# Thresholded attention and a mixer on one core: the queue of double score steps is run over the border between two couples of head pairs, with new ranks for the planner

## The chip, the cores and the metric

The kernel runs on one core of one Trainium2 chip. The metric is the device time of one execution in microseconds (us). A core has TensorE (PE in the profile, with its weight loads as PEld), VectorE (DVE), ScalarE (ACT), GpSimd (POOL) and SyncE (SP), each with its own instruction queue, worked off in order, and DMA queues. PSUM, where PE writes, has eight banks; the kernel names six of them as two "trios" and the last two bank 6 and bank 7.

## The reference, cut to what matters

```python
# q, k, v: (8 batches, 8 heads, 576 rows, 64)
scores = q @ k.T / 8
thresh = max(scores, axis=-1) - tau                       # tau = 0.02
attn = exp(where(scores >= thresh, scores, -1e9) - max(scores))
attn = attn / (sum(attn, axis=-1) + 1e-9)
x = (attn @ v), heads side by side                        # (8, 576, 512)
u = x + (x^T @ U @ V)^T                                   # U: 576 x 32, V: 32 x 576
out = u + relu(u @ w_ch1) @ w_ch2                         # 512 -> 2048 -> 512
```

## The kernel before

**How the work is tiled.** Two heads of one batch make a head pair p; there are 4 in a batch and 32 in all. A *step* is 128 rows of queries against all 576 keys, for both heads of a pair, so it makes two tiles of 128x576. A pair has 576 rows, which is four steps and a half; the two halves of neighbouring pairs p and p+1 (p even) share one step, i = 4. So a couple of pairs has nine steps, and there are 16 couples, 144 steps and 288 tiles.

**What a step does.** `scores` (L574, products at L587) multiplies q and k in fp32 with the array split into quadrants of 64x64, into the two trios. `weigh` (L615, L616, DVE) reads a tile from PSUM, scales it by -1/8, keeps the copy `s_sb` and the row minimum m. `threshold` (L632, ACT) makes the threshold of both tiles, `exponential` (L639, ACT) the exponentials, `select` (L644, L646, DVE) compares, multiplies and sums. The row is completed (`twin`, L664, POOL) and turned, by a DMA (`turn_w`, L670, from SP) or on PE for some early tiles (`turn_pe`, L677, copied out at L687). Then, per pair, `value_tasks` multiplies with v (`product`, L746, L750, L754), joins the parts (L787 ACT, L791 DVE), divides (L798, POOL; for the first four pairs L775 on DVE), goes through the low-rank pair U, V (L811, L826, L833, L874, L881) and turns the result for the mixer (by DMA at L854, by PE at L848 and L896 with copies at L864 and L901).

**Single and double steps.** `score_tasks(*steps)` takes one step or two. One step writes four of the six banks of the trios, two steps write all six (`KEPT`, L149). The `PIECES` (L410) give where the columns are cut, so the instructions of a step are 16 matmul passes in either case. Up to pair 1 all steps are single (`LONE = 2`); from the second couple on the first of nine steps is single and the other eight make four doubles. That is 9 + 15*5 = 84 groups.

**The mixer.** After every fourth pair `mixer_tasks(b)` adds the two layers of batch b: `up` (L930, 16 tasks of four 512-column products), `rest` (L946, for the 64 rows left over of two batches, 128 columns), the rectifier (`relu`, L920, ACT), and `down` (L963, 16 products for each 128 rows of output), then `finish` (L975, DVE) and the stores (L986 to L992, SP and ACT).

**What sets the order.** Nothing runs when it is written: every piece of work is a task with an engine, an estimated cost, dependences and a number of PSUM banks, and `Order.run` (L214 on) places all of them once, at build time, engine by engine. Among the tasks of an engine that could start within a short patience of the first, it takes the one of lowest rank. The rank of most tasks is the planned time at which they became ready plus `OFF[name][phase]`, where the phase is counted by `PHASES = (1, 2, 3, 4, 5, 6, 8, 28)` from the pair's number. Mixer products have a due number instead (`DUE[b]` and what L928 on adds to it): when so many score steps have been placed, they go ahead of all others; until then they are taken only where nothing else is ready. `HOLD` says how long banks are kept free for the next score group. Where PE would stand idle for over 0.45 us of the plan, filler products (L421) of no use to the result are placed, which keep PE's clock up; there are 84 of them.

The loop that lists the tasks stands at the end of the kernel (L1047 on): for every couple it prepares both pairs (loads and turns of q and k), adds the nine score steps, then the values of both, then a mixer where a batch is complete.

Of the kernel before, what the change touches and what calls it, by code (L numbers as in the profile page):

```python
# [81 lines left out]
NT = 5  # L82
# [5 lines left out]
LONE = 2  # L88
# [5 lines left out]
DUE = (461, 86.25, 1468.5, 516.25, 1049.25, 748, 134.75, 1357.5)  # L94
# [33 lines left out]
class Order:  # L128
# [19 lines left out]
    HOLD = (61.76, 61.61, 6.12, 44, 94.32, 94.08, 76.76, 0.01, 9.57)  # L148
# [4 lines left out]
        "copy_main": (25.53, 63.74, -194.99, 34.77, -69.14, 17.14, -324, 37.67, -35.45),  # L153
        "copy_rest": (6.5, -40.06, -14.53, 24.12, -4.13, -20.91, -46.23, 54.32, -95.65),
        "copy_tt": (-16.03, -64.1, 20.85, -110.66, 55.87, 62.18, -42.53, -53.37, -25.08),
        "copy_u": (89.47, -53.33, 162.09, -74.19, 7.13, 9.51, -102.11, -20.31, -73.82),
        "copy_u4": (-5.3, -56.82, -16.18, -6.54, 49.93, -37.52, 64.79, -22.2, -18.99),
        "copy_w": (75.7, -4.79, -22.58, 20.52, -4.75, 68.84, -1.46, 27.15, 10.06),
        "down": (52.39, 32.35, 33.69, 38.82, 7.25, -27.49, 1.69, 19.34, 131.97),
        "exponential": (61.02, 15.66, 97.71, -26.58, 23.56, 95.43, 116.8, 90.08, 11.21),  # L160
        "finish": (-53.17, -45.71, 51.42, 30.79, -14.22, -26.29, 28.78, 16.33, -75.01),
        "first": (-56.79, 75.89, 0.92, -55.7, 35.86, -3.48, 9.68, 53.63, 1.2),
        "high": (-129.72, -35.78, 31.87, -6.58, 48.08, -20.33, -28.95, -46.46, 84.01),
        "inverse": (46.71, -32.89, 54.08, 22.1, 122.91, 38.13, 143.23, 39.39, -23.27),
        "join": (2.19, 36.38, 69.81, -65.72, -28.72, -7.68, -26.75, 24.75, -3.5),
        "load": (14.89, -38.6, -1.87, -55.09, 439, 169.52, 202.43, 266.17, -64.61),
        "low": (23.82, 3.88, -45.02, 6.6, -28.12, -60.17, -87.19, -43.1, 26.46),
        "low4": (64.5, 130.96, 545.14, -26.82, 13.94, -59.21, 35.95, 265.72, -23.85),
        "low_part": (30.38, 13.98, -26.01, -41.71, 130.31, 109.34, -20.82, -133.07, -1.88),
        "low_rank": (-57.69, 16.1, -2.98, 31.4, -60.74, 41.37, 38.61, 8.08, -35.05),  # L170
        "make": (-18.31, -192.85, -81.78, -52.29, 6.69, -18.25, 12.16, -35.09, 27.21),
        "narrow": (5.95, 39.32, -9.64, -6.72, 1.46, 29.45, -10.31, 45.69, -47.12),
        "narrow_u": (-45.99, -94.08, -136.7, -16.38, -46.01, -113.33, 15.29, 42.82, -0.02),
        "narrow_u4": (2.02, -41.08, 15.16, 12.95, 69.79, 35.67, -44.1, -54.14, 56.42),
        "norm": (60.22, 26.73, 14.75, 16.35, 28.89, -20.28, -16.45, 55.02, 19.4),
        "product": (-38.14, -97.33, -17.17, 18.14, -78.98, 56.88, 40.12, 68.18, -110.66),
        "relu": (44.72, -2.34, -31.3, -83.46, 20.06, -116.77, 10.32, 4.5, -36.91),
        "rest": (64.49, 74.43, 34.29, 18.04, -20.78, -41.41, -55.22, -17.62, 44.45),
        "scores": (-2.16, -56.15, 42.01, -69.96, -15.23, -44.76, 4.79, -16.69, -3.93),
        "select": (-41.99, 29.22, -2.51, 135.03, 570.07, 400.28, 184.53, 231.57, 188.34),  # L180
        "send": (43.87, 17.75, 5.67, -19.7, -14.51, -9.84, 285.3, 70.92, -48.56),
        "send_u": (54.83, -57.33, -16.36, 177.37, 12.48, 121.89, 19.74, 60.45, 25.84),
        "spread": (-216.88, 63.66, -12.54, -9.53, -23.32, -1.29, -122.3, 43.34, 63.38),
        "spread4": (12.62, -19.59, -18, 54.22, -34.85, 61.33, -24.98, -50.63, -66.91),
        "spread_v": (-113.69, -64.83, 6.03, 44.27, 73.51, -47.79, -27.38, 65.24, 2.79),
        "sum_u": (-64.77, 3.32, 13.18, 117.53, -78.44, -9.21, 87.33, 127.21, -64.36),
        "sum_u4": (-96.51, 65.77, 2.32, 38.3, 44.64, 21.12, -125.78, 37.98, 23.47),
        "sums": (195.64, 23.57, 47.14, -31.56, 10.32, -16.1, 35.4, 4.49, -58.98),
        "threshold": (-37.94, -91.24, -43.1, -296.86, 94.89, 36.19, 66.3, 1.07, 12.5),
        "turn4": (-36.19, -43.45, 5.14, 7.01, 54.44, -61.28, 52.57, 29.57, -92.54),  # L190
        "turn_main": (0.34, 20.57, 26.79, -161.06, 126.25, -30.36, -38.23, -14.86, -5.97),
        "turn_pe": (-0.48, -21.65, -184.33, 36.36, -95.83, 51.55, 181.65, 20.16, -43.63),
        "turn_rest": (-5.99, -37.64, -0.75, 52.43, -6.2, -61.13, -8.69, -94.49, -32.06),
        "turn_u": (-85.8, -3, -69.47, -45.79, 74.76, -7.02, 3.37, 12.83, 72.77),
        "turn_w": (45.6, -1.19, -137.3, 47.86, -48.09, 10.25, -28.07, -30.73, 72.41),
        "twin": (32.78, -132.71, -13.72, -15.07, -38.22, -14.87, -64, 49.79, 55.76),
# [125 lines left out]
def kernel(  # L322
# [725 lines left out]
    for p in range(0, NP, 2):  # L1048
# [3 lines left out]
        n = 0  # L1052
        while n < 9:
            two = p >= LONE and n
# [44 lines left out]
```

## Time and profile before

| what | value |
|---|---|
| median of 5 runs | 603.32 us (602.52 to 606.07) |
| profiled execution, its own time | 603.32 us |
| its span in the profile | 601.5 us |
| PE, first start and last end in the span | 3.3 and 596.9 us |
| last store issued | 597.6 us |
| granted clock of PE | 0.998 |
| HBM read and written | 37.90 MB and 9.44 MB |

The span goes from the first to the last instruction that the profile holds. A page has six parts: busy time by engine, the span in 40 slices with the busy share of each in tenths, the DMA queues, the chain of work that ended last, the costliest groups of instructions, and the issues of DMAs. The groups give busy time, the mean duration in nanoseconds, then the idle time of the engine just ahead of them with the engine and line that released it. Matmuls overlap in their pipeline, so their durations add up to more than the time that PE spends on them; distances between the starts of neighbours tell that time better.

The chain of work that ended last lies on PE for 54% of the span, on DVE for 9%, on ACT for 4%.

### The profile page before, as it was taken

Reading aid. Unit: us, or ns where it says so; the run is one execution under the profiler, and the core shown is the slowest. Engines: PE = TensorE matmul, PEld = TensorE weight load, DVE = VectorE, ACT = ScalarE, POOL = GpSimd, SP = SyncE. Lnnn points to the kernel's source line nnn. Section 1 sums busy time; section 2 is a strip of 40 time slices with the busy share of each in tenths; the row PEclk is TensorE's granted clock in tenths of the full one; section 3 lists DMA queues with packets and bytes.
Section 4 is the critical chain, followed back from the end, with each engine's and each line's share of the span. In section 5 each row is a group of like instructions: output and inputs, shape, how many; then the busy total and the mean of one; then the engine's idle time right before and its main releaser. Section 6 shows DMA issues by size and latency. Waiting matters only on the chain.

```text
span 601.5 us, 17046 instructions
## 1 busy us (share of the span) xinstructions
PE 580.0 (96%) x6180; PEld 349.9 (58%) x6249; DVE 521.7 (87%) x1399; ACT 458.4 (76%) x959; POOL 371.4 (62%) x596
## 2 busy tenths in 40 slices
PE   7998889999999999999999999999999999999996
PEld 4555665666666556555665656565566666556642
DVE  3989999999999999999988999999999999994101
ACT  4757899998799866896789866897699986784540
POOL 8957587687888864576676665776677633342000
PEclk9999999999999999999999999999999999999999
DMA  7699989957999799989999999887979987667203
GB/s 156 112 180 150 157 146 190 154 117 136 198 193 168 128 185 204 171 145 143 205 154 149 144 182 198 159 161 159 200 153 157 174 152 152 122 95 131 45 1 87
DMA packets 222771, 90.48 MB, mean 150 GB/s; under 512 B 200800, under 2 KB 213040, under 8 KB 222688
## 3 DMA queue, kind: packets, MB, share of 16 engines
q1 hardware_dynamic: 207680, 66.30, 66.3%
q0 software_dynamic: 14048, 22.76, 19.8%
q8 instruction: 49, 0.80, 0.6%
q10 hardware_dynamic: 960, 0.34, 0.2%
q14 instruction: 34, 0.28, 0.2%
HBM read 37.90 MB, written 9.44 MB: 79 GB/s over the span
## 4 chain that ended last, share of the span: by engine, by line
PE 54%; DVE 9%; ACT 4%; issue 3%; SPq 1%; DMA 0%; POOL 0%; DVEq 0%; ACTq 0%
PE trio L587 14%; PE bank L930 8%; PE bank L963 8%; PE bank L750 5%; PE trio L963 5%; PE trio L930 5%; DVE w_ring L646 4%; DVE s_sb L616 3%; ACT e_sb L639 2%; PE bank L946 2%; PE trio L750 1%; PE trio L518 1%; PE bank L518 1%; PE bank L826 1%; PE bank L531 1%
## 5 line engine op out<-in xcount | busy, mean ns | idle before, releaser
L639 ACT ACTIVATE e_sb<-s_sb,m 128x576 bf16<-128x576 f32 x288 | 217.7, 775 | 42.7 <-DVE s_sb L616 32.9
L646 DVE SCALAR_TENSOR_TENSOR w_ring<-s_sb,thr,e_sb 128x576 bf16<-128x576 f32 x288 | 238.5, 858 | 8.7 <-ACT e_sb L639 3.9
L616 DVE TENSOR_SCALAR_CACHE_REDUCE s_sb<-trio 128x576 f32<-128x576 f32 x288 | 203.2, 750 | 16.4 <-PE trio L587 15.1
L587 PE MATMUL trio<-qkT 64*64 64x288 f32 (+2 forms) x2304 | 162.7, 410 | 0.4 <-DVE x L791 0.3
L664 POOL COPY w_ring<-w_ring 128x128 bf16<-128x128 bf16 (+1 forms) x168 | 71.7, 438 | 104.3 <-DVE w_ring L646 82.9
L587 PEld LDWEIGHTS trio<-qkT 64*64 64x64 f32 x2304 | 83.6, 132 | 56.6 <-issue 11.3
L458 POOL DMA_DIRECT2D qkraw<-in_q_dram x125 | 82.3, 665 | 25.9 <-PE bank L518 20.1
L798 POOL TENSOR_TENSOR x<-x,rec 128x256 f32<-128x256 f32 (+1 forms) x84 | 69.6, 830 | 37.1 <-DVE x L791 28.9
L963 PE MATMUL bank<-W2b,R 128*128 128x512 bf16 x347 | 86.1, 379 | 1.5 <-ACT qkT L524 0.3
L963 PEld LDWEIGHTS <-R 128*128 128x128 bf16 x576 | 53.8, 98 | 54.1 <-issue 1.5
L458 POOL DMA_DIRECT2D qkraw<-in_k_dram x125 | 81.4, 659 | 2.8 <-issue 2.2
L930 PE MATMUL bank<-uT,W1b 128*128 128x512 bf16 x304 | 76.5, 379 | 2.4 <-DVE s_sb L616 1.0
L930 PEld LDWEIGHTS <-W1b 128*128 128x128 bf16 x512 | 47.1, 98 | 53.4 <-issue 5.5
L553 POOL TENSOR_TENSOR vh<-vraw_ring,vh 64x128 bf16<-64x128 f32 x64 | 56.1, 877 | 13.6 <-ACT vh L546 6.1
L750 PEld LDWEIGHTS <-wT_ring 128*128 128x128 bf16 x896 | 56.0, 98 | 7.5 <-issue 2.0
L920 ACT ACTIVATE R<-bank 128x512 bf16<-128x512 f32 x91 | 52.5, 594 | 4.8 <-PE bank L930 3.0
L963 PE MATMUL trio<-W2b,R 128*128 128x512 bf16 x197 | 45.8, 379 | 0.5
L930 PE MATMUL trio<-uT,W1b 128*128 128x512 bf16 x172 | 44.1, 379 | 1.5 <-DVE s_sb L616 0.5
L632 ACT ACTIVATE thr<-m,tau_t 128x2 f32<-128x2 f32 x144 | 42.0, 294 | 3.6 <-DVE s_sb L616 3.4
L750 PE MATMUL bank<-vh,wT_ring 128*128 128x128 bf16 x624 | 44.5, 219 | 0.0
L975 DVE TENSOR_TENSOR o<-bank,x 128x512 f32<-128x512 f32 x23 | 15.8, 688 | 32.1 <-PE bank L963 31.9
L746 PE MATMUL bank<-vh,wT_ring 128*128 128x64 bf16 x176 | 33.9, 193 | 0.0
(105 smaller groups left out, 720.1 us busy)
## 6 DMA issues: line engine op xcount, KB each, us to landing
out_dram<-o SPq DMA_DIRECT2D x71, 128.0 KB, 2.8
vraw_ring<-in_v_dram SPq DMA_DIRECT2D x32, 160.0 KB, 3.8
qkraw<-in_k_dram POOLq DMA_DIRECT2D x63, 80.0 KB, 4.2
qkraw<-in_q_dram POOLq DMA_DIRECT2D x62, 80.0 KB, 4.3
vraw_ring<-in_v_dram SPq DMA_DIRECT2D x32, 128.0 KB, 4.0
qkraw<-in_q_dram POOLq DMA_DIRECT2D x63, 64.0 KB, 4.2
qkraw<-in_k_dram POOLq DMA_DIRECT2D x62, 64.0 KB, 4.1
W1b<-in_moe_w_ch_dram POOLq DMA_DIRECT2D x8, 256.0 KB, 6.1
```

The lines of the kernel that those rows point to most:

```text
L458: queue.dma_start(pr.qkraw[part, to, j, :], src[:, j, of, :])
L553: nc.gpsimd.tensor_tensor(out=pr.vh[part, tiles_, :, h, :], in0=raw[part, tiles_], in1=pr.vh[part, tiles_, :, 0, :], op=ALU.subtract)
L587: mm = nc.tensor.matmul(cols[part, lo:hi], a.tT[hs, 0, rows], a.tT[hs, 1, lo:hi], start=True, stop=True)
L616: nc.vector.tensor_scalar(out=s_sb, in0=score_cols(slot, x), scalar1=-scale, scalar2=None, op0=ALU.mult, op1=ALU.min, accum_out=m[:, x:x + 1])
L639: nc.scalar.activation(out=e_sb, in_=s_sb, func=ACT.Exp, bias=m[:, x:x + 1], scale=-1.0)
L646: nc.vector.scalar_tensor_tensor(out=w_sb[:, 0:S], in0=s_sb, scalar=thr_[:, x:x + 1], in1=e_sb, op0=ALU.is_le, op1=ALU.mult, accum_out=pr. ...
L664: nc.gpsimd.tensor_copy(out=w_sb[:, xs, S:640], in_=w_sb[:, xs, 512:S])
L750: nc.tensor.matmul(av[:, 2 * a + j, :], w, pr.vh[:, kt, j, :, :], start=kt == 0, stop=False)
L798: nc.gpsimd.tensor_tensor(out=x, in0=x, in1=over_sum(part), op=ALU.mult)
L920: nc.scalar.activation(out=R2[:, fts, lo:hi], in_=bank[t.got[0]].rearrange("p (f c) -> p f c", c=hi - lo), func=ACT.Relu)
L930: nc.tensor.matmul(bank[t.got[0]], W1b[:, dt, ft * P:(ft + 1) * P], bt.uT[:, dt, :], start=(dt == 0), stop=(dt == 3))
L963: nc.tensor.matmul(ch, R2[:, ft, lo:lo + P], W2b[:, ft, :], start=(ft == 0), stop=(ft == 15))
```

## The change

The list of steps is made a queue. From the third couple on (p > 2) no step is single at the beginning: doubles are taken while more than one step is left, and the one that is left over (`left`) is put together with the first step of the next couple. This group is added when the next couple's first pair has been prepared, and the values of the pair that it completes (`value_tasks(p - 1)`) after it. Couples 3 to 16 so make seven pairs of couples with 9 groups in place of 10, and the groups are 9 + 5 + 7*9 = 77.

With it come new numbers for the planner: all eight of `DUE`, the nine of `HOLD` and all of `OFF`, so that tasks of all kinds change their places in the queues. The kernel's tasks themselves, their instructions and sizes, stay as they are.

```diff
-DUE = (461, 86.25, 1468.5, 516.25, 1049.25, 748, 134.75, 1357.5)
+DUE = (404.5, 221.25, 1360.25, 915.75, 1627.25, 595.75, 216, 1847.5)
...
-    HOLD = (61.76, 61.61, 6.12, 44, 94.32, 94.08, 76.76, 0.01, 9.57)
+    HOLD = (54.85, 52.48, 17.45, 25.61, 65.53, 99.4, 95.02, 0.42, 6.88)
...
     OFF = {
-        "copy_main": (25.53, 63.74, -194.99, 34.77, -69.14, 17.14, -324, 37.67, -35.45),
+        "copy_main": (-16.32, 49.06, 57.41, -61.8, -7.34, 69.61, 49.83, 46.24, 49.14),
...
-        "scores": (-2.16, -56.15, 42.01, -69.96, -15.23, -44.76, 4.79, -16.69, -3.93),
+        "scores": (1.4, 2.34, -57.3, 68.21, -13.54, 72.97, 11.72, -20.31, 98.08),
-        "select": (-41.99, 29.22, -2.51, 135.03, 570.07, 400.28, 184.53, 231.57, 188.34),
+        "select": (-55.63, 147.92, 13.44, 27.66, 832.9, -7.59, 333.09, 234.23, 370.66),
...
-        "weigh": (-145.66, -20.29, -57.18, 79.45, -16.94, 55.31, 45.2, 33.27, 31.94),
+        "weigh": (-74.45, -44.84, 63.82, -70.52, -56.97, 41.56, -44.8, 229.58, 181.08),
...
     weight_loads()
+    left = []
     for p in range(0, NP, 2):
         prepare_tasks(p)
+        nine = [(p, i) for i in range(NT)] + [(p + 1, i) for i in range(4)]
+        if left:
+
+            score_tasks(*left, nine.pop(0))
+            value_tasks(p - 1)
         prepare_tasks(p + 1)
-        nine = [(p, i) for i in range(NT)] + [(p + 1, i) for i in range(4)]
-        n = 0
-        while n < 9:
-            two = p >= LONE and n
-            score_tasks(*nine[n:n + (2 if two else 1)])
-            n += 2 if two else 1
+        while len(nine) > (1 if p > LONE else 0):
+            two = p >= LONE and len(nine) < 9 or p > LONE
+            score_tasks(*[nine.pop(0) for _ in range(2 if two else 1)])
+        left = nine
         value_tasks(p)
-        value_tasks(p + 1)
+        if not left:
+            value_tasks(p + 1)
         if (p + 1) % NPAIR == NPAIR - 1:
             mixer_tasks(p // NPAIR)
```

## The prediction

> **What bounds the kernel now.** I read the page's busy shares first, then its table of slices, then the table of stretches, and last the timelines of single engines.
>
> ```profile
> PE 580.0 (96%) x6180; PEld 349.9 (58%) x6249; DVE 521.7 (87%) x1399; ACT 458.4 (76%) x959; POOL 371.4 (62%) x596
> ...
> PE   7998889999999999999999999999999999999996
> ...
> DVE  3989999999999999999988999999999999994101
> ```
>
> TensorE (PE) is busy over 90% from the seventh slice to the last but one; VectorE (DVE) nearly as long, but it stops after nine tenths of the span. The page warns that a busy PE is not yet PE at its peak, so the stretches come next.
>
> ```profile
> 30.00:60.00 30.00, 27.10 (x368) 16.52 (x367) 25.86 (x75) 19.89 (x39) 20.86 (x36) 1.00 1.14 166
> ...
> 90.00:120.00 30.00, 28.66 (x300) 17.45 (x306) 29.28 (x78) 28.77 (x60) 20.70 (x37) 1.00 1.18 173
> ...
> 180.00:300.00 120.00, 118.42 (x1252) 71.26 (x1267) 114.59 (x305) 94.31 (x202) 80.69 (x126) 1.00 0.94 169
> 300.00:420.00 120.00, 118.57 (x1269) 71.46 (x1285) 114.23 (x306) 96.00 (x208) 81.35 (x124) 1.00 0.92 163
> 420.00:540.00 120.00, 118.51 (x1271) 71.79 (x1286) 118.16 (x316) 98.41 (x207) 64.77 (x100) 1.00 0.88 153
> 540.00:601.50 61.50, 56.54 (x383) 30.39 (x387) 14.39 (x29) 22.56 (x44) 4.58 (x9) 0.98 0.33 65
> ```
>
> Columns: stretch, its length, then busy time of PE, weight loads, DVE, ScalarE (ACT) and GpSimd (POOL) with instruction counts, granted clock (full), DMA. Between 180 and 540 us PE lacks 4.5 us of 360, DVE 13. Between 90 and 120 DVE and ACT are the fuller ones.
>
> Is that busy PE also working at its full rate? I added up the PE instructions in program order, each at the distance between two starts that its kind keeps when nothing holds it: 0.216 us for 512 columns, 0.056 for 128, 0.028 for 64, 0.109 and 0.165 for the fp32 transposes, and score groups as priced below. The sum is 570.4 us, of which 84 filler products are 18.1. PE starts at 3.3 us and ends at 596.9, so the idle time left in it is 26.5, the 3.3 included. Set against the start times of the score groups, this lag is 6.1 us at the first group, 20.9 at step 36 (134.0 us), 21.0 at step 43 (164.7 us), 26.0 at step 142 (532.0 us). So **PE loses 15 us in the first 130 us and only 5.6 in the 460 us after that**: from then on the time is the number of PE's instructions, and a microsecond of PE work removed there is a microsecond of time.
>
> **The merged groups.** The score products run with the array split in quadrants (64*64 in the rows). The timeline of PE shows what such a group costs alone and doubled:
>
> ```profile
> 269.12 1.89 PE L930 MATMUL bank<-uT,W1b 128*128 128x512 bf16 x7
> 270.94 1.20 PE L587 MATMUL trio<-qkT 64*64 64x288 f32 x16
> 272.07 0.40 PE L750 MATMUL bank<-vh,wT 128*128 128x128 bf16 x4
> ...
> 435.24 1.03 PE L963 MATMUL bank<-W2b,R 128*128 128x512 bf16 x4
> 436.20 2.17 PE L587 MATMUL trio<-qkT 64*64 64x288 f32 x32
> 438.30 0.33 PE L531 MATMUL bank<-ident,qkraw 128*128 128x128 f32 x1
> ```
>
> A group of one step (x16) takes 272.07-270.94 = 1.13 us to the next start, one of two steps (x32) 438.30-436.20 = 2.10. Entry costs more: four 512-column products from 435.24 would end at 436.10 and the group begins at 436.20, so about 0.09. Two singles cost 2*(1.13+0.09) = 2.44, a double 2.10+0.09 = 2.19: 0.25 per merger. The built program has 60 double and 24 single groups before, 67 and 10 after: fourteen singles became seven doubles, **7*0.25 = 1.8 us of PE work saved**. All fourteen lie behind step 18, nearly all where PE is the bound. Every other kind of PE instruction is as numerous as before, the 84 fillers too, and so is everything on DVE, ACT, POOL and the DMA queues; the sum for the new order is 568.6. The last step of one couple now waits for the q and k of the next couple's first pair; these lie in the other buffer of two and were due one group later anyway, so I see no lack of input.
>
> Here a rule speaks against the change. The page shows DVE waiting 15.1 us for score products in all (the line of L616), 5 of it behind 165 us, and the DVE needs 0.68 us (start to start) for each of the four 128x576 tiles that a double group leaves: 2.7 us against PE's 2.1. The Trainium skill, "TensorEngine Tiling (Array Packing)", section "PSUM Bottleneck", says that tiling hastens TensorE but not the emptying of PSUM, which can then become the bottleneck; by that the merger would give nothing. By the row PE has other work for those 2.7 us, and gains the 1.8.
>
> **The new ranks** move nearly everything. I weighed them by position in the built order, in three places.
> - *Early, where PE has idle time.* Up to step 36 the new order has PE 1.6 us further in real work (fillers left out), but DVE 2.6 us further as well when it reaches that step's scores. Idle time of PE changes by the second less the first, were DVE alone to set the pace: +1.0. At other steps: +1.9 at step 32, -2.0 at 42, -1.9 at 60. On the average of steps 10 to 70 about nothing. Bounds -2.0 and +1.9; I take -0.5, the sign of steps 46 to 62, which are the last before PE has no more gaps.
> - *Middle.* From step 70 to 120 PE has done 2 to 4 us less at the same place of DVE's list (4.3 at step 86): mixer products are put off, since none of the new due numbers falls within the 144 steps (two of the old ones do, 86.25 and 134.75). If PE stays the bound this costs nothing, the scores merely come earlier. If DVE can't follow, PE waits: bounds 0 and +4.3. DVE's spare time between 180 and 420 us is 5.4 + 5.8 = 11.2 us, more than twice that; I take 0.
> - *Tail.* Behind the last score group 63 us of PE work follow in the new order (65.2 with the group, 64.4 before), the same three blocks last: 64 small first-layer products, 64 large ones, 80 of the second layer, 34.7 us. The gap to them changes:
>
> ```profile
> 561.12 0.22 PE bank L896 x4
> 561.34 0.86 PE bank L963 x4
> 562.21 0.89 PE bank L946 x16
> ```
>
> This piece of the chain of waits shows four products of L963 lying over the copy of the turned rows (L901, 561.38 to 561.96 in ACT's timeline), which L946 needs. In the new order three fillers stand there, 0.65 us, and the four products come earlier. From the start of the transposes to L946 the chain needs 1.09; transposes and fillers fill 0.22+0.65, so 0.2 is lost (the fillers are in the 568.6 already). The second-layer products ahead of the transposes are 12 in place of 8, so this chain's beginning is covered better than before.
>
> **The sum.** -1.8 (groups) - 0.5 (early) + 0 (middle) + 0.2 (tail) = -2.1 us. The profiled execution took 603.32 with a span of 601.5; the median of the five runs is the same 603.32. Forecast 601.3, about 0.34% less. A measurement of this kernel can tell about 0.5%, 3.0 us, from no change, so this is called no change though I expect the sign to show.
>
> **Rivals.**
> 1. *The new order also closes gaps of PE.* For it: at steps 42 to 62, where the gaps end, PE is up to 2.0 us better placed; and of the 5.6 us lost after 134 us about a third goes with entries and waits at score groups that are now fewer. Against it: as many fillers as before, so the planner saw as much idle time. Price: -1.8 - 2.0 - 1.0 = -4.8, **598.5**. That PE's start also improves would give at most 2 more.
> 2. *Score groups wait for DVE: slower.* A double group needs six banks of PSUM emptied, a single four. Where DVE is late, the group's products stand at the head of PE's queue, and all the mixer products behind them stand too. Place: steps 70 to 120 (about 260 to 450 us), where the new order has PE up to 4.3 us short of work at the same place of DVE's list, and the seven borders, where DVE has two more tiles to empty, 2*0.68 = 1.4 each, 9.5 in all. Price between 4.3 and 9.5; with 6 in the middle, 603.3 - 1.8 + 0.2 + 6 = **607.7**. It decides from the point at which PE's idle time ahead of L587 (0.4 us on the page) passes some 4.6 us. Against it: DVE's 11 us of spare time. For it: in the whole span DVE loses time to stretched instructions; L646 takes 0.74 us start to start undisturbed, and 1.09 at 100.44 in DVE's timeline.
> 3. *The change does not do what it says.* The groups are counted in the built program, so only their price can fail: if entry costs were hidden by something else, the gain is 0 instead of 1.8, **603.1** by the other terms. It lies inside the forecast's band.
>
> ```profile
> L616 DVE TENSOR_SCALAR_CACHE_REDUCE s_sb<-trio 128x576 f32<-128x576 f32 x288 | 203.2, 750 | 16.4 <-PE trio L587 15.1
> L587 PE MATMUL trio<-qkT 64*64 64x288 f32 (+2 forms) x2304 | 162.7, 410 | 0.4 <-DVE x L791 0.3
> ```
>
> ```profile
> 100.44 1.16 DVE L646 SCALAR_TENSOR_TENSOR w_ring<-s_sb,thr,e_sb 128x576 bf16<-128x576 f32 x1
> ```
>
> The first fence has two of the page's groups (busy, mean ns, idle ahead of them and its releaser), the second one stretched instruction from DVE's timeline.
>
> **How the numbers follow.** The forecast's band, within 3 us of 603.3, with the third rival inside: 0.45. The first rival: 0.36. The second: 0.19. Faster by over 0.5%: 0.36; within: 0.45; slower: 0.19. The forecast's own range is -1.8 with the early bounds and the tail, 599.7 to 603.6. For 8 in 10 I reach down to the first rival with its last 2 us, 596.5, and up into the second, short of its middle, to 606.5.
>
> **What would show it.** In the profile after: pieces x32 and x16 of L587 still at 2.10 and 1.13; PE starts its last block 34.7 us before its end; the lag of PE's starts behind its summed work is near 21 at step 43 and 26 at the end. If the time falls by more than 3 us, the lag at step 43 must be under 20. If it rises, idle time of PE ahead of L587 or L930 must have risen by microseconds, with DVE as releaser, and DVE must be at 119 us or more of 120 in the middle stretches. What would prove the reasoning wrong altogether is a changed time with the same lag, or a changed price of PE's instructions: those counts and prices are the base of the sum.

## The result and the profile after

The changed kernel takes **607.6 us** (median of 43 runs, 603.32 to 617.33), the kernel before beside it 604.81 (80 runs, 601.56 to 610.82). The ratio is **1.0035, 95% interval 1.0020 to 1.0051**: slower by some 2.1 us, less than the 0.5% that were called "no change", but with the wrong sign, and the median lies above my range; set on the 603.32 of the prediction, the ratio makes 605.4, above the forecast's own 603.6 and inside the 8-in-10 range. The execution profiled with the result was a disturbed one (613.49 us), so the lines below are from another profile of the same program, `after_3` (604.72 us, span 602.9), itself one of its faster executions.

The page, busy time and slices; then the stretches that I had shown of before (busy time of PE, weight loads, DVE, ACT and POOL with counts, granted clock, DMA):

```profile
PE 584.8 (97%) x6249; PEld 351.8 (58%) x6249; DVE 520.0 (86%) x1399; ACT 461.7 (77%) x959; POOL 366.6 (61%) x596
...
PE   7988889999999999999999999999999999999996
...
DVE  4869999899998999999998999989999999994201
```

```profile
30.00:60.00 30.00, 26.61 (x370) 18.05 (x369) 24.18 (x69) 21.04 (x41) 19.00 (x36) 0.94 1.08 161
...
90.00:120.00 30.00, 29.36 (x312) 17.20 (x310) 28.31 (x81) 28.50 (x58) 21.23 (x37) 1.00 1.25 159
...
180.00:300.00 120.00, 119.66 (x1293) 71.97 (x1285) 115.75 (x313) 97.11 (x206) 80.10 (x126) 1.00 0.99 167
300.00:420.00 120.00, 119.08 (x1290) 72.81 (x1291) 112.60 (x303) 98.44 (x210) 81.18 (x124) 1.00 0.95 165
420.00:540.00 120.00, 119.90 (x1302) 72.19 (x1295) 117.07 (x318) 99.79 (x209) 65.07 (x101) 1.00 0.87 154
```

In the middle PE is fuller than before and DVE has 14.6 of 360 us to spare. What stands out is the first of these lines: DVE 24.2 us of 30 in place of 25.9, and a granted clock of 0.94 in place of 1.00. The timeline of PE has the price of the pieces, and the place ahead of L946:

```profile
434.87 2.75 PE L963 MATMUL bank<-W2b,R 128*128 128x512 bf16 x12
437.55 2.17 PE L587 MATMUL trio<-qkT 64*64 64x288 f32 x32
439.66 0.33 PE L531 MATMUL bank<-ident,qkraw 128*128 128x128 f32 x1
```

```profile
562.48 0.39 PE L896 MATMUL bank<-identb,ub 128*128 128x128 bf16 x4
562.70 0.81 PE L421 MATMUL trio<-identb 128*128 128x512 bf16 x3
563.54 1.05 PE L946 MATMUL bank<-uT,W1b 128*128 128x128 bf16 x16
```

A double group still takes 439.66-437.55 = 2.11, and the tail is as forecast: 1.06 from the transposes to L946, three fillers between, 34.8 us from there to the end of PE. Two groups of the page:

```profile
L616 DVE TENSOR_SCALAR_CACHE_REDUCE s_sb<-trio 128x576 f32<-128x576 f32 x288 | 204.2, 749 | 16.6 <-PE trio L587 15.0
L587 PE MATMUL trio<-qkT 64*64 64x288 f32 (+2 forms) x2304 | 162.2, 409 | 1.7 <-DVE s_sb L616 1.6
```

PE's idle time ahead of L587 rose from 0.4 to 1.7, nearly all of it one wait. So where did the time come from? The lag of PE's starts behind its summed work (570.38 us before, 568.58 after), group by group, tells it:

| lag at step, us | 8 | 14 | 21 or 22 | 30 | 42 or 43 | 142 |
|---|---|---|---|---|---|---|
| before (603.32) | 9.6 | 12.1 | 17.0 | 19.6 | 21.0 | 26.0 |
| before_2 (605.99) | 9.1 | 11.3 | 19.6 | 22.3 | 23.7 | 28.7 |
| after (613.49) | 8.2 | 22.1 | 27.7 | 29.5 | 32.9 | 38.3 |
| after_2 (606.24) | 8.4 | 15.1 | 21.4 | 23.1 | 26.6 | 31.1 |
| after_3 (604.72) | 7.9 | 14.6 | 20.2 | 22.0 | 25.4 | 29.6 |
| after_4 (611.72) | 8.5 | 21.2 | 26.8 | 28.7 | 32.2 | 36.6 |

Two things differ. From step 8 to 14 the old order loses 2.2 to 2.5 us, the new one 6.7 to 13.9. From step 30 to 42 the old order loses 1.4, the new one 3.4 to 3.5. Between them the old order is not free either: from step 14 to 21 before_2 loses 8.3 us, with a wait of 2.7 us for turned rows and half clock from 71.69 to 75.10; before loses 4.9. Behind step 42 the old loses 5.0, the new 4.2 to 5.4. The spread of the new order goes with the transfers: between 30 and 70 us the turned rows (`wT_ring`) landed in 8.2 and 7.9 us (median) in after and after_4, whose lags at step 14 are 22.1 and 21.2, and in 4.0 and 4.1 in after_2 and after_3, with 15.1 and 14.6. But in before and before_2 they took 6.1 and 6.6, and the old order lost 2.5 and 2.2 from step 8 to 14: slow transfers alone do not make the loss, but in the new order the loss is larger with them. After_3 against before: -1.8 of work, +3.6 of lag, -0.3 behind the last group, so PE ends 1.5 later (598.35 and 596.86).

### The profile page after: what moved, and what is told of

It reads as the page before. It is cut to its first block, busy times and chain, and to the rows that moved or that the text cites. A ratio compares the mean times of both kernels' runs of the same rounds, so it can differ in the third digit from the quotient of the medians.

```text
span 611.7 us, 17037 instructions
## 1 busy us (share of the span) xinstructions
PE 582.4 (95%) x6181; PEld 351.9 (58%) x6249; DVE 519.4 (85%) x1399; ACT 461.8 (75%) x959; POOL 366.0 (60%) x596
## 4 chain that ended last, share of the span: by engine, by line
PE 56%; DVE 13%; ACT 8%; issue 5%; DMA 3%; POOL 2%; DVEq 0%; ACTq 0%; POOLq 0%
PE trio L587 13%; PE bank L930 8%; PE bank L963 8%; PE trio L963 6%; PE bank L750 6%; DVE w_ring L646 6%; PE trio L930 4%; DVE s_sb L616 4%; ACT e_sb L639 3%; DMA wT_ring<-w_ring 1%; PE trio L518 1%; PE bank L946 1%; PE bank L518 1%; DVE o L975 1%; DMA wT<-w_ring 1%
## 5 line engine op out<-in xcount | busy, mean ns | idle before, releaser
L646 DVE SCALAR_TENSOR_TENSOR w_ring<-s_sb,thr,e_sb 128x576 bf16<-128x576 f32 x288 | 235.0, 847 | 13.3 <-DMA wT_ring<-w_ring 9.3
L616 DVE TENSOR_SCALAR_CACHE_REDUCE s_sb<-trio 128x576 f32<-128x576 f32 x288 | 204.1, 748 | 19.0 <-PE trio L587 17.4
L587 PE MATMUL trio<-qkT 64*64 64x288 f32 (+2 forms) x2304 | 164.3, 413 | 1.4 <-DVE s_sb L616 1.2
L664 POOL COPY w_ring<-w_ring 128x128 bf16<-128x128 bf16 (+1 forms) x168 | 74.0, 450 | 103.4 <-DVE w_ring L646 80.2
L587 PEld LDWEIGHTS trio<-qkT 64*64 64x64 f32 x2304 | 84.8, 134 | 57.4 <-issue 10.2
L798 POOL TENSOR_TENSOR x<-x,rec 128x256 f32<-128x256 f32 (+1 forms) x84 | 57.9, 690 | 63.5 <-DVE x L791 46.1
L963 PE MATMUL bank<-W2b,R 128*128 128x512 bf16 x329 | 81.1, 379 | 1.8 <-ACT qkT L524 0.5
L930 PE MATMUL bank<-uT,W1b 128*128 128x512 bf16 x318 | 80.1, 379 | 0.8
L930 PEld LDWEIGHTS <-W1b 128*128 128x128 bf16 x512 | 47.7, 98 | 50.5 <-DVE s_sb L616 1.6
L553 POOL TENSOR_TENSOR vh<-vraw_ring,vh 64x128 bf16<-64x128 f32 x64 | 60.1, 939 | 13.4 <-ACT vh L546 7.7
L750 PEld LDWEIGHTS <-wT_ring 128*128 128x128 bf16 x896 | 56.0, 98 | 15.1 <-issue 7.9
L750 PE MATMUL bank<-vh,wT_ring 128*128 128x128 bf16 x752 | 54.1, 219 | 1.1 <-DMA wT_ring<-w_ring 1.1
L963 PE MATMUL trio<-W2b,R 128*128 128x512 bf16 x214 | 50.8, 379 | 0.5
L930 PE MATMUL trio<-uT,W1b 128*128 128x512 bf16 x161 | 41.5, 379 | 1.7 <-DVE s_sb L616 0.6
L975 DVE TENSOR_TENSOR o<-bank,x 128x512 f32<-128x512 f32 x22 | 15.1, 686 | 31.0 <-PE bank L963 27.4
L746 PE MATMUL bank<-vh,wT_ring 128*128 128x64 bf16 x208 | 40.2, 193 | 0.0
```

What stands on the lines that cost most here:

```text
L553: nc.gpsimd.tensor_tensor(out=pr.vh[part, tiles_, :, h, :], in0=raw[part, tiles_], in1=pr.vh[part, tiles_, :, 0, :], op=ALU.subtract)
L587: mm = nc.tensor.matmul(cols[part, lo:hi], a.tT[hs, 0, rows], a.tT[hs, 1, lo:hi], start=True, stop=True)
L616: nc.vector.tensor_scalar(out=s_sb, in0=score_cols(slot, x), scalar1=-scale, scalar2=None, op0=ALU.mult, op1=ALU.min, accum_out=m[:, x:x + 1])
L646: nc.vector.scalar_tensor_tensor(out=w_sb[:, 0:S], in0=s_sb, scalar=thr_[:, x:x + 1], in1=e_sb, op0=ALU.is_le, op1=ALU.mult, accum_out=pr. ...
L664: nc.gpsimd.tensor_copy(out=w_sb[:, xs, S:640], in_=w_sb[:, xs, 512:S])
L750: nc.tensor.matmul(av[:, 2 * a + j, :], w, pr.vh[:, kt, j, :, :], start=kt == 0, stop=False)
```

## The experiments

"Theory A" began as: the loss sits in the first 160 us, at PE tasks that the new order has moved ahead of what they wait for. Its rivals are named run by run. For single moves I wrote the order of the planner out as a literal list, so that one task can be moved and all others stay; these profiles have other line numbers (L536 for L421, L702 for L587, L731 for L616, L861 for L746, L869 for L754, L792 for L677, L926 for L811).

**The same kernels again.** No edit.

> The changed kernel once more, for a second profile. Theory C (most of the loss is PE's idle time in the first 130 us, which differs from run to run with the landing of turned rows and with the half clock that follows a long wait): PE's lag behind its summed work at step 46 differs by several us from the first profile's 33.5, its growth from step 46 to the end does not (4.8), and the time goes with the lag. Theory B (merged groups wait for DVE): the growth behind step 46 is what is over that of the kernel before (5.5).

> The kernel before once more, for a second profile. Theory C: its lag at step 43 differs from the first profile's 21.0 as well, if its time does; the growth from there to the end is 5 to 6 us again.

> The changed kernel a third time, for a third profile. Same expectations as for the second.

> The changed kernel as it is, on the same chip as the three kernels with one task moved, so that they can be set against it. Theory A and B alike: ratio 1.001 to 1.004 to the kernel before, PE's wait ahead of score group 8 between 1.1 and 1.6 us; half clock behind it where the wait is 1.5 us or more.

Measured: after_2 606.2 us, ratio 1.0013 (0.9986 to 1.0039), and after_4 607.6, ratio 1.0054 (1.0021 to 1.0086), 12 runs each; single runs of 605.99 (before) and 604.72 (after). The lags are in the table. After_4 missed what was expected of it: its ratio is higher, and group 8 did not wait. DVE was never at 119 of 120 in the middle (117.08 at most in the four profiles), and the growth behind step 42 is hardly larger than before: the second rival (score groups wait for DVE, steps 70 to 120) is out. That its 607.7 stands beside the median of 607.6 is luck; it was set on 603.3, and the loss does not lie at its place.

**The price of a switch of the array.** One 128-column product of the full array between the two steps of each of the 60 double groups of the kernel before; its result is not used.

```diff
 for slot, (p, i) in enumerate(steps):
+    if slot:
+        nc.tensor.matmul(trio[0][:, 1376:1504], identb, identb, start=True, stop=True)
```

> The kernel before, with one 128-column product of the whole array put between the two steps of each of its 60 double score groups, into columns of the trio that nobody reads. If the price of a group holds (entry 0.09 us, and 0.16 that a second step costs less inside a double) and PE is the bound, each costs 0.06 + 0.09 + 0.16 = 0.31 us: 60 of them 18 us, of which those before 130 us (11 of the 60) may be hidden: 15 to 18 us, a ratio of 1.025 to 1.031. If switching between quadrants and the whole array is hidden beside DVE's work, under 3 us.

Measured: 618.79 us, ratio 1.0226 (1.0188 to 1.0264), 4 runs, 13.7 us more: 0.23 for each of the 60, 0.28 if only the 49 behind step 36 count. That is under the 15 to 18 expected. The price itself is there in PE's timeline of this run:

```profile
269.71 1.20 PE L589 MATMUL trio<-qkT 64*64 64x288 f32 x16
270.84 0.23 PE L578 MATMUL trio<-identb 128*128 128x128 bf16 x1
271.00 1.20 PE L589 MATMUL trio<-qkT 64*64 64x224 f32 x16
272.13 0.33 PE L531 MATMUL bank<-ident,qkraw 128*128 128x128 f32 x1
```

The group takes 272.13-269.71 = 2.42 in place of 2.10, so 0.32, as expected (0.31). So the 0.25 per merger holds as work of PE, but of the 19 us put in (60 times 0.32) only 13.7 are paid, seven tenths: idle time that PE had took up the rest (the lag at step 142 is 4.6 us smaller than in before). On the time, seven mergers would then be worth less than 1.8, some 1.2 to 1.5 (0.23 or 0.28, less the product's own 0.06, seven times; an estimate).

**Halves of both orders.** hy_ba_16 has the old order up to the group of step 16, then the new; hy_ab_16 the reverse. No task changes, only the list; the fillers go with it, 90 in hy_ba_16 and 78 in hy_ab_16 in place of 84, so that PE has 1.3 us more work in the one and 1.3 less in the other.

> The order of the kernel before up to the score group of steps 16 and 17 (some 65 us), from there on the order of the changed kernel with its merged groups. Theory A: the loss is all in the first part and the merged groups keep their 1.8 us: 0.994 to 0.998 of before. Theory B: 1.002 to 1.005, like the changed kernel.

> The opposite: the order of the changed kernel up to the score group of steps 16 and 17, from there on that of the kernel before with its 84 groups. Theory A: the loss of the first part stays and the 1.8 us of the mergers go: 1.004 to 1.009 of before. Theory B: 0.999 to 1.001.

Measured: hy_ba_16 609.59, ratio 1.0076 (1.0048 to 1.0104); hy_ab_16 605.89, ratio 1.0018 (0.9988 to 1.0049). Both missed what theory A expected of them, hy_ba_16 by more than its fillers explain: the seam of hy_ba_16 itself loses (9.8 between steps 14 and 22, against 5), with two stretches of half clock. But from step 30 to 42 hy_ba_16 loses 3.5 like the new order, hy_ab_16 1.4 like the old. So that part goes with the order there, not with what came before.

**Two first guesses at the early waits.** x1 puts the products of pair 1, rows 256 to 511 (they waited 4.3 us for rows turned by DMA in the first profile after), and what hangs on them behind group 14. x2 issues two of the W1 loads some 35 us later, to ease the transfers.

```diff
 PE, x1:  turn_pe,
-product (pair 1, rows 256-511),
 scores 12, ..., scores 14,
+product (pair 1, rows 256-511), and its low-rank tasks
```

> The order of the changed kernel, written down as a list, with one thing moved: the fifth product with v (pair 1, rows 256 to 511) and what hangs on it stand behind the score group of steps 14 and 15 instead of ahead of that of steps 12 and 13. Theory A (that product waits for a DMA that turns the rows, ahead of two score groups in PE's queue, and the wait varies with the DMA traffic): about 4 us less than the changed kernel, 0.995 to 0.999 of before, and no wait of PE for a turned row over 1.5 us between 45 and 70 us. Theory B (merged score groups wait for DVE, all along the middle): no different from the changed kernel, 1.002 to 1.005 of before.

> The order of the changed kernel with two of the eight loads of the first-layer weights (256 KB each) issued about 35 us later, from after 75 us; nothing else moves. Theory A, with DMA traffic as the cause of the late rows: 1 to 4 us less than the changed kernel, 0.996 to 1.002 of before, rows land earlier between 45 and 60 us. If rows are late because SyncE issues them late, or theory B: no difference, 1.002 to 1.005.

Measured: 611.56 us, ratio 1.0093 (1.0061 to 1.0126), and 615.19, ratio 1.0102 (1.0043 to 1.0160). Both missed: in x1 the long wait for the DMA is gone, but the lag jumps 7.0 between steps 14 and 16 in its place; in x2 PE waited 7.2 us for turned rows later on and ran at half clock for 10.2 us. Between 30 and 70 us the turned rows landed in 3.9 us (median) in x2, as in after_2 and after_3, which have the W1 loads early: that fewer such loads make the rows come sooner is not shown.

**One place in detail: score group 8.** In PE's queue the old order has 16 fillers, the products of pair 0 (rows 0 to 255), then group 8; the new one 18 fillers, group 8, turns of the next pair, then these products. Timelines of DVE and PE in after_3 (start, duration, in brackets idle time and releaser):

```profile
33.77 0.82 DVE L646 SCALAR_TENSOR_TENSOR w_ring<-s_sb,thr,e_sb 128x576 bf16<-128x576 f32 x1 [4.11 <-DMA wT_ring<-w_ring]
34.51 0.08 DVE L646 DVE_READ_ACCUMULATOR w_ring<-s_sb,thr,e_sb 128x1 f32 x1
34.51 0.81 DVE L646 SCALAR_TENSOR_TENSOR w_ring<-s_sb,thr,e_sb 128x576 bf16<-128x576 f32 x1
35.25 0.08 DVE L646 DVE_READ_ACCUMULATOR w_ring<-s_sb,thr,e_sb 128x1 f32 x1
35.25 0.75 DVE L616 TENSOR_SCALAR_CACHE_REDUCE s_sb<-trio 128x576 f32<-128x576 f32 x1
```

```profile
33.78 0.70 PE L587 MATMUL trio<-qkT 64*64 64x288 f32 x4
36.07 1.19 PE L587 MATMUL trio<-qkT 64*64 64x288 f32 x12 [1.58 <-DVE s_sb L616]
37.18 1.74 PE L518 MATMUL bank<-ident,qkraw 128*128 128x128 f32 x8
38.72 0.63 PE L754 MATMUL trio<-vh,wT_ring 128*128 128x64 bf16 x8
39.16 0.24 PE L746 MATMUL trio<-vh,wT_ring 128*128 128x64 bf16 x1
```

And PE in the kernel before:

```profile
33.58 0.40 PE L754 MATMUL bank<-vh,wT_ring 128*128 128x64 bf16 x8
33.81 0.19 PE L746 MATMUL bank<-vh,wT_ring 128*128 128x64 bf16 x1
35.22 0.41 PE L754 MATMUL bank<-vh,wT_ring 128*128 128x64 bf16 x8 [1.21 <-DMA wT_ring<-w_ring]
...
35.84 1.20 PE L587 MATMUL trio<-qkT 64*64 64x288 f32 x16
```

In after_3 DVE's L646 may not write into `w_ring` before the DMA has turned the old rows; the L616 behind it, whose reading frees the bank for group 8, comes 4.1 us late; the group has issued 4 of 16 products and stands, and the products of pair 0, of which the old order had done half by 33.8 us, stand behind it. Then PE is slow: eight transposes take 38.72-37.18 = 1.54 in place of 8*0.109 = 0.87, nine products with v 0.48 in place of 0.26. The clock records give half clock from 37.47 to 40.88. Three kernels test the place: x3 moves the products back ahead of the group, x4 leaves all and adds useless work, x5 puts this one part of the new order into the old.

```diff
 PE, x3:  18 fillers,
+product (pair 0, rows 0-255),
 scores 8, turn_main, turn_main,
-product (pair 0, rows 0-255),

 PE, x4:
-18 fillers, scores 8
+26 fillers, scores 8

 PE, x5 (in the old order):  16 fillers,
-product (pair 0, rows 0-255),
 scores 8, turn_main, turn_main,
+product (pair 0, rows 0-255),
```

> The new order with one task moved: the products of pair 0, rows 0 to 255 (L754, 1.04 us of PE) stand ahead of score group 8 in PE's queue, as in the old order, in place of behind it; the 18 fillers stay ahead of both. Theory A (the loss sits at this place: PE has score group 8 at the head of its queue, waits 1.5 us for VectorE, which waits for a transfer to release w_ring, and is then granted half the clock for 3.4 us, 1.7 us more): the wait falls to under 0.8 us, no half clock follows, the lag at step 14 falls from 14.6 to 15.1 to 11.5 to 13, and the time to 1.5 to 3 us under the changed kernel's, ratio to the kernel before 0.996 to 0.999. Theory B (VectorE sets the pace up to step 36, so PE's time here is given back a few steps later): the wait goes but the lag at step 38 stays at 25 to 26.5 and the time within 0.7 us of the changed kernel's.

> The new order with nothing moved, and 8 more filler products (1.73 us of useless PE work) ahead of score group 8, where PE waits. Theory A, half-clock part: the group starts when it did, PE's idle time there falls under 0.3 us, no half clock follows at 37 to 41 us, and the time falls by 1 to 2 us against the changed kernel, though PE has more work. Theory B: time the same or up to 1.7 us longer.

> The old order with this one part of the new: the products of pair 0, rows 0 to 255, moved behind score group 8 (with the old 84 groups, none merged). Theory A: PE waits 1 to 2 us ahead of score group 8, half clock follows for 3.4 us, the lag at step 14 rises from 11.3 to 12.1 to 14 to 15.5, and the time is 1.5 to 3 us over the kernel before, ratio 1.003 to 1.005. Theory B: ratio 0.999 to 1.001.

Measured on one chip, 11 or 12 runs each, with ratios to the kernel before: after_4 607.6, 1.0054; **x3 605.72, 1.0017 (0.9985 to 1.0048); x4 605.89, 1.0019 (0.9993 to 1.0045); x5 606.72, 1.0021 (0.9997 to 1.0046)**. By the medians x3 and x4 are 1.9 and 1.7 us under the changed kernel on this chip and x5 1.8 over the kernel before: the signs that theory A gave. But the intervals of these pairs overlap, x3's ratio misses the 0.996 to 0.999 and x5's the 1.003 to 1.005 of theory A, and after_2, the changed kernel itself, had 1.0013 on another chip. So the times settle neither the size nor the sign; what is shown is in the profiles. In x5's own profile PE waits only 1.19 ahead of group 8, no half clock follows, and the lag at step 14 is 12.9, short of the 14 to 15.5 expected; its extra time came later in that execution. PE's timeline of x4:

```profile
31.74 5.78 PE L536 MATMUL trio<-identb 128*128 128x512 bf16 x26
37.44 1.20 PE L702 MATMUL trio<-qkT 64*64 64x288 f32 x16
38.58 1.09 PE L633 MATMUL bank<-ident,qkraw 128*128 128x128 f32 x8
```

The eight transposes behind the group last 0.93 to the next start (39.51), the clock stays full, and 1.73 us of useless work has cost nothing that shows. But the lag at step 42 is 24.8 in x3 and 24.1 in x4, without any half clock, against 21.0 in before and 23.7 in before_2: what theory A had of step 14 (11.5 to 13) was missed in x3 (14.1). The wait and the half clock at this place are real and are not all. In after_4 group 8 did not wait at all; there it was the next such place:

```profile
54.79 0.19 PE L746 MATMUL bank<-vh,wT_ring 128*128 128x64 bf16 x1
58.64 0.61 PE L754 MATMUL bank<-vh,wT_ring 128*128 128x64 bf16 x8 [3.65 <-DMA wT_ring<-w_ring]
59.06 0.24 PE L746 MATMUL bank<-vh,wT_ring 128*128 128x64 bf16 x1
59.11 0.61 PE L754 MATMUL bank<-vh,wT_ring 128*128 128x64 bf16 x8
59.54 0.24 PE L746 MATMUL bank<-vh,wT_ring 128*128 128x64 bf16 x1
59.71 4.12 PE L587 MATMUL trio<-qkT 64*64 64x288 f32 x32
```

Products of pair 1 wait 3.65 us for a transfer, and the double group behind them takes 4.05 to the next start (63.76) in place of 2.10, at half clock from 57.50 to 64.33.

**Both places mended.** x6 is x3 with these products of pair 1 behind group 12 in place of ahead of it.

```diff
 PE, x6:  18 fillers,
+product (pair 0, rows 0-255),
 scores 8, ..., turn_pe,
-product (pair 1, rows 256-511),
 scores 12,
+product (pair 1, rows 256-511),
```

> The new order with both places mended: the products of pair 0, rows 0 to 255, ahead of score group 8, and the products of pair 1, rows 256 to 511 (the one that waited 4.3 and 3.6 us for transposed rows in two profiles of the changed kernel), behind score group 12 in place of ahead of it. Nothing else moves. Theory A (the loss is these two waits with the half clock that follows them, and some 2 us between steps 30 and 42 that this doesn't touch): no PE wait over 1.5 us and no half clock before 60 us, lag at step 14 12 to 13.5 and at the end 28 to 29.5, the time 2 to 3.5 us under the changed kernel's, ratio to the kernel before 0.997 to 1.000. Theory B (these waits only move on to the next instruction that needs the same transfers): lag at step 16 as in the changed kernel, 16 or more, ratio 1.001 to 1.005.

Measured: 606.37 us, ratio 1.0046 (1.0018 to 1.0074): theory A missed. The lag at step 12 is 13.0, but at step 14 16.9. The timeline of PE shows the loss one link further on in the chain of the same pair, its low-rank product, as theory B had it:

```profile
55.83 0.19 PE L861 MATMUL bank<-vh,wT_ring 128*128 128x64 bf16 x1
57.35 0.44 PE L926 MATMUL bank<-xb_ring,Ub 128*128 128x128 bf16 x5 [1.33 <-ACT xb_ring L918]
...
59.53 3.09 PE L536 MATMUL trio<-identb 128*128 128x512 bf16 x7
62.56 1.88 PE L702 MATMUL trio<-qkT 64*64 64x288 f32 x28
```

PE stands for 1.5 us from the last start to the next, less the product's own 0.03 (the view has 1.33 of it as idle), and seven fillers behind it take 62.56-59.53 = 3.03 in place of 1.51: half clock again, from 58.98 to 62.40 by the records.

**The gaps between steps 30 and 42.** In all profiles with this part of the new order (after and its repeats, x1, x3, x4, x6, hy_ba_16) the lag grows there by 3.4 or 3.5, in all with the old (before and its repeat, x5, hy_ab_16) by 1.4. After_3 has three waits of this kind, two of them here:

```profile
138.07 2.17 PE L587 MATMUL trio<-qkT 64*64 64x288 f32 x32
140.17 0.33 PE L531 MATMUL bank<-ident,qkraw 128*128 128x128 f32 x1
140.33 0.60 PE L518 MATMUL bank<-ident,qkraw 128*128 128x128 f32 x4
141.44 0.45 PE L811 MATMUL trio<-xb_ring,Ub 128*128 128x128 bf16 x5 [0.51 <-DVE s_sb L616]
```

```profile
131.58 0.45 PE L677 MATMUL trio<-identb,w_ring 128*128 128x128 bf16 x5
132.50 1.02 PE L963 MATMUL bank<-W2b,R 128*128 128x512 bf16 x4 [0.47 <-ACT qkT L524]
```

The double group holds six banks; two short transposes take the other two within 0.6 us; the third task needs a bank that DVE or ACT has yet to empty. x7 moves three long tasks behind these groups and gives the short ones beside them other banks; x8 adds x3.

```diff
 PE, x7:
-up 11, scores 30, turn_main, low_rank (bank 6), turn_pe (bank 0)
+scores 30, turn_main, up 11, low_rank (bank 0), turn_pe (bank 3)
...
-product 18, scores 34, turn_main, low_rank (bank 6), turn_pe (bank 0)
+scores 34, turn_main, product 18, low_rank (bank 0), turn_pe (bank 3)
...
-product 23, ..., scores 36, turn_rest (bank 6), turn_main, low_rank (bank 0), turn_pe (bank 6)
+scores 36, turn_main, product 23, turn_rest (bank 0), low_rank (bank 3), turn_pe (bank 1)
```

> The new order with three long PE tasks moved from ahead of a double score group to behind it (four first-layer products, L930, behind group 30; one set of mixer products each, L750 and L746, behind groups 34 and 36), and the short tasks beside them in other PSUM banks. Theory D (between steps 30 and 42 PE stands three times, 0.5 to 0.7 us each, right behind a double group: that group holds six of the eight banks, two short tasks of 0.3 to 0.5 us take the other two, and the third has to wait until VectorE or ScalarE has emptied one): the three gaps go, the lag grows by 1.6 to 2.3 us from step 30 to 42 in place of 3.4 to 3.5, nothing of it comes back behind step 42, and the time is 1 to 1.8 us under the changed kernel's, ratio to the kernel before 0.999 to 1.003. Theory E (PE waits there because VectorE and ScalarE are the fuller engines; a gap closed opens ahead of the next group): growth 3 us or more, ratio 1.002 to 1.006.

> The same, and the products of pair 0, rows 0 to 255, ahead of score group 8 as well. Theory D and the place at group 8 together: lag at step 42 22.5 to 24 in place of 24.8 to 26.6, at the end 27.5 to 29, the time 602.5 to 604.5, ratio 0.997 to 1.001. Theory E: ratio 1.001 to 1.004, as with that task alone.

Measured: 610.90, ratio 1.0111 (1.0081 to 1.0142), and 609.67, ratio 1.0095 (1.0065 to 1.0126). Theory D missed, and the ratios lie above theory E's as well: the lag now grows by 7.1 and 7.2 from step 30 to 42, where E had 3 or more. PE's timeline of x7:

```profile
131.07 0.19 PE L861 MATMUL bank<-vh,wT_ring 128*128 128x64 bf16 x1
132.86 0.45 PE L926 MATMUL trio<-xb_ring,Ub 128*128 128x128 bf16 x5 [1.60 <-ACT qkT L639]
133.54 0.45 PE L792 MATMUL trio<-identb,w_ring 128*128 128x128 bf16 x5 [0.22 <-DVE s_sb L731]
...
143.61 0.45 PE L926 MATMUL trio<-xb_ring,Ub 128*128 128x128 bf16 x5 [1.21 <-DVE s_sb L731]
144.29 0.45 PE L792 MATMUL trio<-identb,w_ring 128*128 128x128 bf16 x5 [0.22 <-DVE s_sb L731]
```

The low-rank products, which I had put into a bank of the group, now wait 1.6 and 1.2 us for it although 1.5 us of other work stands ahead of them: DVE comes to these tiles later than I took it to. That a wait for banks of the group can cost PE microseconds here is shown; that the three gaps are the whole 2.0 us is not, since my remedy changed banks and places at once.

**The mergers without the new ranks.** m_first and m_last keep the old order on every engine and merge only, the merged group standing where its first or its second step stood; PSUM banks had to be given anew at 96 and 92 places, and in m_first 107 tasks of DVE move by up to 5 places. n_oldrank_newloop has the loop of the change and the old ranks, and lets the planner order them.

```diff
 m_first, order of score groups:
-18 | 19 20 | 21 22 | 23 24 | 25 26 | 27 | 28 29
+18 19 | 20 21 | 22 23 | 24 25 | 26 27 | 28 29

 n_oldrank_newloop:  the change's last hunk alone; DUE, HOLD, OFF as before
```

> The mergers alone: 67 double and 10 single score groups, and every other task of the five engines in the order of the kernel before (VectorE's tasks up to 5 places moved, since a merged border brings the second step's scores earlier; PSUM banks are given anew; the 84 fillers stay where they were). A double group stands where the old order had its first step. Theory A (the mergers are worth the 1.8 us worked out, and the new ranks lose 3 to 4 us before step 42): lag at step 14 as before (11 to 12.5), at step 42 21 to 24, at the end 26 to 29 like the kernel before, and the time 1 to 2.5 us under the kernel before, ratio 0.996 to 0.9985. Theory C (merging itself is what costs: PE waits for six banks in place of four, and nothing is won): the lag grows by 1.8 us or more over the seven borders against the kernel before, ratio 1.000 to 1.004.

> The mergers alone as in the run beside it, but a double group stands where the old order had its second step, so VectorE keeps its old order and gets the scores of the seven border steps later. Theory A: between the kernel before and the other variant, ratio 0.997 to 1.001, as VectorE may wait for score products at the borders. Theory C: ratio 1.001 to 1.005.

> The loop of the change alone: the border steps are merged, the planner plans with the old ranks and due numbers. It places 113 fillers in place of 84, 6.3 us more of PE work, so the work sum is 574.8. If the new ranks were a mere loss beside a gain of 1.8 by merging, this would take 601.5. Theory A (ranks and loop belong together: merged groups ask for six banks of PSUM at a border, and the old ranks send PE into waits there): the fillers show the idle time that the planner saw, the time is 608 to 620, ratio 1.008 to 1.025.

Measured: m_first 651.58, ratio 1.0774 (1.0737 to 1.0811); m_last 694.88, 1.1481 (1.1432 to 1.1530); n_oldrank_newloop 621.30, 1.0280 (1.0225 to 1.0335). The last kernel does not compute the reference's result, so I use it for its order of size only. It is far off the 601.5 of new ranks that are a mere loss, and just over theory A's 608 to 620. The first two are off every forecast: in m_first PE is busy 114.6, 114.1 and 114.4 of 120 us in the three middle stretches and waits 17 times for DVE ahead of a score group. So nothing here shows the merged groups gaining without an order and banks of their own; that the new ranks are what they need is argued. What of the 47 us in m_first is the merging and what the banks given anew isn't separated by these runs.

## Why the prediction was wrong, point by point

- **The bound (held in the main).** Most of PE's work in the middle is paid in time: 13.7 us for 60 inserted switches of 0.32 each, seven tenths of them, or nearly nine tenths if the eleven up to step 36 cost nothing; and a lag that grows hardly faster in the new order behind step 42 (4.2 to 5.4 against 5.0). That all of it is paid, microsecond for microsecond, is a little too much.
- **The merged groups, -1.8 (held as work of PE).** A double takes 2.11, the work sum is 568.58, an inserted switch takes 0.32 on the timeline and 0.23 to 0.28 of the time. What the mergers alone are worth in time no run shows. For the rule of the Trainium skill that I weighed there, "TensorEngine Tiling (Array Packing)", section "PSUM Bottleneck": in the middle nothing of it shows (PE's idle time ahead of L587 is 1.7 us in all of after_3, 1.6 of it at 34.5 us); waits for banks behind and ahead of score groups did appear, but between steps 8 and 42, behind a double group at the short tasks around it.
- **Early, -0.5 with bounds -2.0 and +1.9 (failed).** This is the step of the prediction that failed: that PE's idle time in the first part would change by -0.5. In its place the lag at step 42 is 4.4 us larger than before in after_3 and 11.9 in the first profile; even in x3, which had no half clock, it is 3.8 larger than in before, which had none either, and 1.1 larger than in before_2, which had. I see three errors in my working; the waits are shown, that these errors make the whole is argued. I averaged differences of position over the steps, but a lag once lost is not won back: what counts is the sum of the waits. I compared PE's list with DVE's alone, while the waits measured are for transfers of turned rows (group 8, the products of pair 1) and for PSUM banks behind double groups (steps 30 to 42, 2.0 of the 4.4). And I priced an idle microsecond of PE at one: behind such a wait PE may run 3.41 us or more at half clock, 1.7 us again.
- **Middle, 0 (held).** From step 42 to the end the lag grows 4.2 to 5.4, before 5.0; DVE has 14.6 us to spare. The point of decision of the second rival, 4.6 us ahead of L587, was not reached (1.7, and that in the first 40 us). So my sign for a rise, idle time of PE by microseconds ahead of L587 or L930 with DVE at 119 us of 120, did not come although the time rose: in after_4, with 611.72 us, PE's idle time ahead of L587 is 0.2.
- **Tail, +0.2 (held).** 1.06 from transposes to L946, 0.87 of it filled.
- **The sum.** In after_3: -1.8 of work, +4.4 of lag by step 42, -0.8 behind it, so the last score group starts 1.8 later than before, PE ends 1.5 later, and the time is 1.4 longer. Over all runs it is +2.1 (1.2 to 3.1), which with -1.8 of work leaves about +4 for the early part.

How much of it is the clock? Of the executions of before 51 of 115 show a granted clock of 0.999 or more, too high for even one stretch of 3.41 us at half clock, and they average 603.65 us; of the changed kernel 18 of 65, averaging 605.4. So some 1.7 us stay without half clock, by waits. That the rest comes from falling to half clock more often fits, but a clock under 0.999 is a rough sign: the first profile of before has 0.998 from half clock behind the end of PE's work alone.

What stays open: which single edit of the new order would win back the 2.0 us between steps 30 and 42 (x7 made them worse), and why the wait of the early part falls now on group 8, now on the products of pair 1, in executions of one program; the transfers' own timing differs, and nothing I moved is shown to have steadied it. Open too is whether the mergers would gain with an order that keeps the old lag before step 42. No version here beats the kernel before.

## What to carry to other kernels

A price per instruction, read from the timeline, can be checked by inserting the instruction (here 0.32 for a forecast 0.31), but even on the busiest engine not all of it need show in the time (here seven tenths). What a re-ordering does to the part where the busiest engine still has gaps can't be priced like that, and a saving of 0.3% is smaller than it. When a planner's list is new, walk through the queue of the busiest engine where it still waits and ask at each head of the queue what it waits for, transfers and PSUM banks included, and what finished work stands behind it. Where a short wait of PE can't be avoided, useless products in it can keep the clock full at no cost that shows, as in x4; that they save time was not clear of the noise here.

## What the runs showed of the hardware

- While PE still has work, half clock comes in stretches of 3.41, 6.83 and 10.24 us, whole multiples of 3.41, behind a time in which PE was idle: a wait of 1.33 us by the view (x6), 1.54 (after_2), 1.58 (after_3), 1.86 (x2), 3.65 (after_4). The length of a wait alone does not decide: 1.83 in x1, which lay over the border of two such stretches (0.2 and 1.6), was followed by none, nor was one of 1.19, nor this one in after_3, which lay inside one stretch (81.84 to 85.25, counted on from 37.47):

```profile
84.99 0.40 PE L848 MATMUL bank<-identb,ub 128*128 128x128 bf16 x4 [1.62 <-ACT ub L840]
```

- The Trainium skill, "TensorE: Matmul & The Clock Gate", Part 1, gives the same window, 3.4 us, and half clock after at least one idle window; here an idle of under half a window (1.71 us) was enough in x6, after_2 and after_3, and the 1.62 us just shown were not.
- The DMA that turns rows ended at 33.28 us in before and 33.77 in after_3 at the same place of DVE's list, though DVE came to it 0.8 us earlier in after_3 (its waits are 2.83 and 4.11): working ahead on DVE brought nothing there, since the transfer set the time.
